# A new PE/DVE schedule for a fused linear-attention and softmax-attention kernel: exp pattern 2,2, background matmuls in pairs on a credit, a pool of free banks, and "warmer" matmuls

## Chip, cores, metric

One core of one Trainium2 chip. The metric is the device time of one execution in microseconds (us). The kernel before took 1404.0 us (median of 6 runs, 1399.91 to 1411.62).

Words used below: PE is the matmul engine, ACT the engine that does exp, DVE the vector engine, POOL the fourth engine. "Clock" is the granted TensorE clock as the profile gives it, as a share of full speed. In the traces of this case it is only ever 0.5 or 1.0, so a mean of 0.59 means 18% of the time at full clock. A "bank" is one of the eight buffers of 128 x 512 results that the matmuls write to; a "flow" is one sequence of background steps; a "unit" is the work of four heads on 512 queries; PV is the product of the exps with V; M0pad in the prediction is the tile of the bound for the exps, which enters the score matmul as its 17th row.

## The reference, cut to what matters

```python
# A: linear attention,  B: softmax attention; S=2048, D=512, H=32 heads of Dh=16 each
def _A_ref(x, wqkv, wo):
    q, k, v = ...                                   # x @ wqkv, by heads
    phi = lambda t: jnp.where(t > 0, t + 1, jnp.exp(t)) + 1e-6
    kv = einsum(phi(k), v); z = phi(k).sum over s
    return (phi(q) @ kv / (phi(q) @ z + 1e-6)) @ wo
def _B_ref(x, wqkv, wo):
    scores = einsum("bhqd,bhkd->bhqk", q, k) * Dh ** -0.5
    return (softmax(scores) @ v) @ wo
return concatenate([A, B], axis=-1)
```

B needs 32 x 2048 x 2048 exps, and the kernel has ACT do them. A and the projections are "background".

## The kernel before

The heads of B are handled in 8 groups of four. The scores are computed in tiles of 128 keys by 512 queries (2048 tiles). A score matmul contracts only 17 rows, so the four heads of a group sit in the four 32-row strips of the PE array, and their matmuls run at the same time. ACT takes the exp of 3 and of 2 score banks in turn. A PV group is four matmuls, each 32 columns of the array wide, also at the same time. The program decides once and for all in which order PE gets score, PV and background matmuls.

```python
NSC = 5                       # score banks
ACT_PATTERN = (3, 2)          # banks per exp
MISC_BANKS = tuple(range(NSC + 1, 8))     # two free banks for everything else
PE_BUDGET = 700.0; DVE_BUDGET = 1000.0
...
def make_S(n):                # one score tile: K=17 rows of strip j
    add("pe", mm(pf(b), KaT[32*j:32*j+17, gs, 128*kb:128*(kb+1)],
                 QaT[32*j:32*j+17, gs, 512*qb:512*(qb+1)], tp=(32*j, 0)), ...)
def make_PV(m):               # four matmuls, 32 columns each, into the accumulator bank
    ...
    if kb == NKB - 1:         # end of a unit (32 in all): evict, then the fp32 finish "fin"
        copy_task("dve", accs[:, u2, :], pf(ACC_BANK), ...)
        fin_flow[u] = start_flow(fin(g, qb, u), 0)
...
def prep(g):                  # background: K, Q, V of a later group, and a bound for the exps
    for t in range(4):
        yield (900.0, 650.0)                    # declared PE and DVE cost of the next step
        b = misc_bank()
        add("pe", _seq([mm(pf(b), wkp[:, gs, c, :], xTB[:, c, 512*t:512*(t+1)],
                        start=(c == 0), stop=(c == 3)) for c in range(4)]), ...)   # four in a row
    ...
    tt("pool", m0_f[...], prod[...], half_f[...], ALU.pow, ...)    # square root on POOL
...
def pump(scale):              # after each exp: let background flows go on
    pe_b = PE_BUDGET * scale; dve_b = DVE_BUDGET * scale
    fresh = True
    for f in list(flows):
        c = f["cost"]
        if (c[0] <= pe_b and c[1] <= dve_b) or fresh:   # the first step is always let through
            ...
            step_flow(f)
...
for i in range(NA):           # the main loop, one exp per turn
    add("act", exp of the next 3 or 2 banks)
    make_S(...)  ; make_PV(...) ; pump(ln / 3.0)
```

## Time and profile before

| | before |
|---|---|
| span of the profiled run | 1398.0 us |
| mean granted clock | 0.592 |
| PE / ACT / DVE / POOL busy | 79% / 71% / 20% / 15% |

First, lines of the profile page: the busy time and share of each engine; then the span in 40 slices, where a digit is tenths of busy time and PEclk is the clock in tenths; then the chain of work that ended last; then three groups of instructions (line, engine, operation, output<-inputs, shapes, count | busy us, mean ns of one | idle time before them and what ended it).

```profile
span 1398.0 us, 14809 instructions
PE 1109.4 (79%) x6520; PEld 362.2 (26%) x6520; DVE 280.7 (20%) x554; ACT 988.1 (71%) x875; POOL 212.3 (15%) x147
...
ACT  2265665675565667887688768887688768887885
...
PEclk8665555575565575555555565556555665555777
...
PE 46%; ACT 34%; POOL 10%; DVE 8%; issue 2%; ACTq 0%; POOLq 0%
...
L810 ACT ACTIVATE ring<-ps 128x1536 bf16<-128x1536 f32 (+1 forms) x819 | 959.8, 1250 | 275.9 <-PE ps L292 275.0
L292 PE MATMUL ps<-QaT,KaT 17*128 17x512 bf16 x2048 | 461.9, 561 | 166.1 <-ACT ring L810 165.9
...
L334 POOL TENSOR_TENSOR m_f<-prod,half_f 128x16 f32<-128x16 f32 x32 | 92.9, 2902 | 9.4 <-DVE prod L334 7.7
```

Neither ACT nor PE is full on average, and the clock is at half for most of the time. The average hides two stages. In a quiet stretch, without background, the timeline (start us, length us, engine, what; merged where contiguous) shows this:

```profile
739.17 5.57 ACT L810 ACTIVATE ring<-ps 128x1024 bf16<-128x1024 f32 x5
...
741.62 0.61 PE L292 MATMUL ps<-QaT,KaT 17*128 17x512 bf16 x3 [0.56 <-ACT ring L810]
...
742.16 0.62 PE L292 MATMUL ps<-ring,Va 128*32 128x512 bf16 x4
...
742.71 0.61 PE L292 MATMUL ps<-QaT,KaT 17*128 17x512 bf16 x2
...
743.88 0.61 PE L292 MATMUL ps<-QaT,KaT 17*128 17x512 bf16 x3 [0.56 <-ACT ring L810]
```

Here ACT runs without a gap, and PE, although at half clock, waits for it. Five tiles take 2.26 us (741.62 to 743.88). Count PE by the distance from start to start, since the ends overlap: a group of score matmuls holds PE for 0.54 us and a PV group for 0.55. With background it is PE that lacks time (PE alone, the clock rises within this stretch):

```profile
290.03 0.62 PE L292 MATMUL ps<-ring,Va 128*32 128x512 bf16 x4
290.58 1.89 PE L292 MATMUL ps<-xTB,wkp 128*128 128x512 bf16 x4
292.40 0.61 PE L292 MATMUL ps<-QaT,KaT 17*128 17x512 bf16 x3
292.94 0.62 PE L292 MATMUL ps<-ring,Va 128*32 128x512 bf16 x4
...
296.15 0.40 PE L292 MATMUL ps<-ring,Va 128*32 128x512 bf16 x4
296.48 1.04 PE L292 MATMUL ps<-xTB,wkp 128*128 128x512 bf16 x4
297.45 0.39 PE L292 MATMUL ps<-QaT,KaT 17*128 17x512 bf16 x2
297.77 1.21 PE L296 MATMUL ps<-ident_bf,arena 128*128 128x128 bf16 x16
```

At half clock four background matmuls hold PE for 1.82 us (290.58 to 292.40); at full clock 0.97 (296.48 to 297.45), PV 0.33 and scores 0.32. The clock is thus worth a factor of 1.7 to 1.9 on these three.

When does the clock rise? The Trainium skill ("TensorE: Matmul & The Clock Gate", Part 1, the HAM clock gate) says that PE's clock is halved by default and released after a busy window of 3413 ns, a window that runs freely. The clock records of this trace agree: only 0.5 and 1.0 occur, in multiples of 3413 ns. That part does not say what counts as busy. So I added up, for each such window of the trace, the columns that the matmuls streamed, weighted by the share of the array that they use (17 of 128 rows for a score matmul, 32 of 128 columns for a PV matmul, fp32 double), and divided by what full rate would have streamed. The weights and the threshold are a fit; the table has the windows of the loop, from the first score to the last PV:

| work of the window, share of full rate | windows (before) | of which the next window ran at full clock |
|---|---|---|
| under 0.34 | 299 | 0 |
| 0.34 to 0.36 | 19 | 0 |
| 0.36 to 0.38 | 12 | 8 |
| over 0.38 | 55 | 55 |

### The profile page before, as it was taken

Reading aid. Unit: us, or ns where it says so; the run is one execution under the profiler, and the core shown is the slowest. Engines: PE = TensorE matmul, PEld = TensorE weight load, DVE = VectorE, ACT = ScalarE, POOL = GpSimd, SP = SyncE. Lnnn points to the kernel's source line nnn. Section 1 sums busy time; section 2 is a strip of 40 time slices with the busy share of each in tenths; the row PEclk is TensorE's granted clock in tenths of the full one; section 3 lists DMA queues with packets and bytes.
Section 4 is the critical chain, followed back from the end, with each engine's and each line's share of the span. In section 5 each row is a group of like instructions: output and inputs, shape, how many; then the busy total and the mean of one; then the engine's idle time right before and its main releaser. Section 6 shows DMA issues by size and latency. Waiting matters only on the chain.

```text
span 1398.0 us, 14809 instructions
## 1 busy us (share of the span) xinstructions
PE 1109.4 (79%) x6520; PEld 362.2 (26%) x6520; DVE 280.7 (20%) x554; ACT 988.1 (71%) x875; POOL 212.3 (15%) x147
## 2 busy tenths in 40 slices
PE   5588787787888888778777877778777877778887
PEld 3223222233233233222312222222222232122222
DVE  6333222232244331002100110002100210000111
ACT  2265665675565667887688768887688768887885
POOL 4641111124100032001400050003200140000000
PEclk8665555575565575555555565556555665555777
DMA  7000000000000000000000000000000000000000
GB/s 241 1 1 0 1 0 0 0 1 0 0 14 17 24 8 1 0 0 0 1 1 0 1 1 0 0 1 1 0 1 0 1 1 0 0 0 8 16 16 23
DMA packets 11056, 13.53 MB, mean 10 GB/s; under 512 B 752, under 2 KB 9968, under 8 KB 10992
## 3 DMA queue, kind: packets, MB, share of 16 engines
q1 hardware_dynamic: 10992, 12.59, 2.6%
q8 instruction: 51, 0.84, 0.2%
q14 instruction: 13, 0.11, 0.0%
HBM read 8.39 MB, written 4.19 MB: 9 GB/s over the span
## 4 chain that ended last, share of the span: by engine, by line
PE 46%; ACT 34%; POOL 10%; DVE 8%; issue 2%; ACTq 0%; POOLq 0%
PE ps L292 42%; ACT ring L810 33%; POOL m_f L334 7%; PE ps L296 4%; DVE accs L302 2%; POOL qsq L334 1%; DVE tmpU L328 1%; POOL ksq L334 1%; ACT tmpE L343 1%; DVE o_tok L334 1%; DVE RlPad L302 1%; POOL M0pad L330 1%; DVE KaT L320 0%; DVE rden L340 0%; DVE rl_tok L340 0%
## 5 line engine op out<-in xcount | busy, mean ns | idle before, releaser
L810 ACT ACTIVATE ring<-ps 128x1536 bf16<-128x1536 f32 (+1 forms) x819 | 959.8, 1250 | 275.9 <-PE ps L292 275.0
L292 PE MATMUL ps<-QaT,KaT 17*128 17x512 bf16 x2048 | 461.9, 561 | 166.1 <-ACT ring L810 165.9
L292 PE MATMUL ps<-ring,Va 128*32 128x512 bf16 x2048 | 296.3, 570 | 1.0 <-ACT ring L810 1.0
L292 PEld LDWEIGHTS ps<-QaT,KaT 17*128 17x128 bf16 x2048 | 83.8, 98 | 497.8 <-ACT ring L810 434.8
L334 POOL TENSOR_TENSOR ksq<-KaT 128x1024 bf16<-128x1024 bf16 x16 | 30.2, 1892 | 625.6 <-DVE KaT L320 625.6
L302 DVE COPY accs<-ps 128x512 f32<-128x512 f32 x32 | 22.1, 691 | 489.2 <-PE ps L292 489.2
L292 PEld LDWEIGHTS ps<-ring,Va 128*32 128x32 bf16 x2048 | 56.1, 100 | 208.2 <-issue 206.2
L334 POOL TENSOR_TENSOR m_f<-prod,half_f 128x16 f32<-128x16 f32 x32 | 92.9, 2902 | 9.4 <-DVE prod L334 7.7
L292 PE MATMUL ps<-esel_f,accs 128*128 128x4 f32 x256 | 59.0, 354 | 26.2 <-DVE accs L302 26.2
L343 ACT ACTIVATE tmpE<-tmpU 128x512 f32<-128x512 f32 x32 | 20.1, 629 | 83.8 <-DVE tmpU L328 83.8
L292 PEld LDWEIGHTS ps<-esel_f,accs 128*128 128x128 f32 x256 | 56.2, 324 | 41.8 <-DVE accs L302 41.8
L292 PE MATMUL ps<-wA,arena 128*128 128x512 bf16 x128 | 55.3, 581 | 0.7 <-DVE kvacc L334 0.7
L292 PE MATMUL ps<-xTB,wqp 128*128 128x512 bf16 x128 | 45.5, 496 | 0.8 <-DVE o_tok L334 0.8
L292 PE MATMUL ps<-xTB,wkp 128*128 128x512 bf16 x128 | 45.1, 495 | 0.0
L296 PE MATMUL ps<-ident_bf,M0pad 128*128 128x128 bf16 x128 | 19.1, 304 | 30.8 <-POOL M0pad L330 30.8
L334 POOL TENSOR_TENSOR qsq<-QaT 128x1024 bf16<-128x1024 bf16 x16 | 30.2, 1892 | 70.7 <-DVE QaT L302 70.7
L296 PE MATMUL ps<-ident_f,RlPad 128*128 128x128 f32 x128 | 35.2, 430 | 5.9 <-DVE RlPad L302 5.9
L334 POOL TENSOR_TENSOR pk_n<-tmpW,tmpE 128x512 bf16<-128x512 f32 x16 | 20.2, 1262 | 128.4 <-ACT tmpE L343 128.3
L328 DVE TENSOR_SCALAR tmpU<-ps 128x512 f32<-128x512 f32 x32 | 22.1, 692 | 81.8 <-PE ps L292 81.8
L292 PE MATMUL ps<-wopad,arena 128*128 128x512 bf16 x128 | 37.4, 431 | 0.0
L334 POOL TENSOR_TENSOR pqT<-tmpW,tmpE 128x512 bf16<-128x512 f32 x16 | 20.2, 1263 | 86.8 <-ACT tmpE L343 80.4
L320 DVE TENSOR_SCALAR KaT<-ps,negc 128x512 bf16<-128x512 f32 x30 | 22.5, 751 | 46.2 <-PE ps L292 46.2
(102 smaller groups left out, 578.2 us busy)
## 6 DMA issues: line engine op xcount, KB each, us to landing
arena<-in_B_x_dram SPq DMA_DIRECT2D x4, 512.0 KB, 5.5
arena<-in_A_x_dram SPq DMA_DIRECT2D x4, 512.0 KB, 7.9
out_dram<-stA SPq DMA_DIRECT2D x16, 128.0 KB, 1.7
out_dram<-stB SPq DMA_DIRECT2D x16, 128.0 KB, 1.7
wB<-in_B_wqkv_dram SPq DMA_DIRECT2D x1, 1536.0 KB, 10.4
wA<-in_A_wqkv_dram SPq DMA_DIRECT2D x1, 1536.0 KB, 11.9
wopad<-in_B_wo_dram SPq DMA_DIRECT2D x4, 128.0 KB, 2.7
woA<-in_A_wo_dram SPq DMA_DIRECT2D x1, 512.0 KB, 3.6
```

Of the source, the lines that this page charges most:

```text
L292: return lambda e: e.matmul(o, l, r_, start=start, stop=stop, tile_position=tp, skip_group_check=sgc)
L296: return lambda e: e.transpose(o, i, ident)
L302: em = lambda e: e.tensor_copy(out=o, in_=i)
L320: em = lambda e: e.tensor_scalar(out=o, in0=i, scalar1=vec, scalar2=None, op0=ALU.add)
L328: em = lambda e: e.tensor_scalar(out=o, in0=i, scalar1=s1, scalar2=s2, op0=op0)
L330: em = lambda e: e.tensor_scalar(out=o, in0=i, scalar1=s1, scalar2=s2, op0=op0, op1=op1)
L334: return add(eng, lambda e: e.tensor_tensor(out=o, in0=i0, in1=i1, op=op), **kw)
L343: return add("act", lambda e: e.activation(out=o, in_=i, func=func), **kw)
L810: add("act", lambda e, b0=b0, ln=ln, rp=rp: e.activation(out=ring[:, 512 * rp:512 * (rp + ln)], in_=ps[:, 512 * b0:512 * (b0 + ln)], func= ...
```

## The change

The intent: at every exp, give PE exactly as much background as fits beside the exp, by a cost model that puts a 512-column matmul at 216 ns (the commonest distance between the starts of two such matmuls at full clock in the trace before); keep a third bank free; take the square root from POOL to DVE; and fill idle PE time with matmuls on zero weights ("warmers"), to keep its clock up. The core of the diff:

```diff
-NSC = 5
-ACT_PATTERN = (3, 2)
-RING = 10
+NSC = 4
+ACT_PATTERN = (2, 2)
+RING = 8
-PE_BUDGET = 700.0
-DVE_BUDGET = 1000.0
+T_EXP = {1: 490.0, 2: 916.5, 3: 1343.5, 4: 1770.0}
+T_MM = 216.0
+T_SLAT = 110.0
+PE_MARGIN = 100.0
+PE_MAX_BURST = 520.0
+PE_TARGET = 0.62
+DVE_SHARE = 0.9
...   # banks: try_bank / acquire / release instead of misc_bank, a flow waits until one is free
+        def pe_group(b, fs, r, per=2, cost=T_MM):     # a row of matmuls, cut into pairs
+            for k in range(0, len(fs), per):
+                if not first: yield (cost * len(ch), 0.0)
+                add("pe", _seq(ch), ...)
...   # prep: K, Q, V first, then the bound; the square root without POOL
-                tt("pool", m0_f[...], prod[...], half_f[...], ALU.pow, ...)
+            ts("dve", sq_y0[:].bitcast(I32), prod[:].bitcast(I32), 0.5, 532487669.0, ...)
+            recip(sq_r[:], sq_y0[:], ...)             # one Newton step
+            ...
...
+        def pump(pe_avail, dve_avail):
+            credit["pe"] = min(credit["pe"] + pe_avail, PE_MAX_BURST)
+            ...   # a step only goes if its cost is covered by the credit
+        def warmers(k):
+            if not acc_state["open"]: return
+            for _ in range(k):                        # adds zero to the open accumulator
+                add("pe", mm(pf(ACC_BANK), zeros_bf[:], xTB[:, 0, 0:512], start=False, stop=False,
+                             sgc=True), ...)
...
-            pump(ln / 3.0)
+            used = pump(t_per - main - PE_MARGIN, DVE_SHARE * t_per)
+            idle = PE_TARGET * t_per - main - used
+            if idle > 0.5 * T_MM:
+                warmers(int(idle / T_MM + 0.5))
```

Here `main` is 326 for a step with scores and 216 more with PV. A step without PV gets 490 of credit, one with PV 274, and the cap is 520. So one pair (432) goes per two steps, and a warmer comes only into a step with neither PV nor background.

## The prediction

> **What bounds the kernel now.** The span is 1398 us at a mean clock of 0.592 (list of cores). The page shows PE busy 79%, ACT 71%; the chain of waits is PE 46%, ACT 34%. The exp evictions cost 1461 ns (1536 columns) and 1038 ns (1024) and overlap by about 120 ns, so ACT alone would need some 926 us. In quiet groups (timeline, 741 to 755 us) ACT is at that floor, 2.26 us per five tiles, even at clock 0.50. The rest is bound by PE at half clock: a group of score matmuls holds PE for 0.54 us, a group of four PV matmuls 0.55, four 512-column background matmuls 1.82; at full clock they take 0.32, 0.33 and 0.97.
>
> **When the clock rises.** The Trainium skill ("TensorE: Matmul & The Clock Gate", the HAM clock gate) says that the clock is halved unless PE was busy in a free-running window of 3413 ns. The trace shows the same two states and window. Sorting the windows by matmul work (columns, weighted by the share of array cells used: a 17-row score matmul 0.13, a 32-column PV matmul 0.25) the next window ran at full clock where the work reached about 0.36 of full rate, and at half clock below, with few exceptions. Score and PV groups alone (about 0.2) never reach it.
>
> **What the change does.**
> - Pattern 3,2 becomes 2,2: 1024 score groups instead of 819. ACT floor 926 to 939 us (estimate). PE at half clock: 205 x 0.54 = 110 us more.
> - Background is cut into pairs, one pair per two steps, on credits that assume the full clock (216 ns). Two steps of score, pair, score, PV cost at half clock 0.54 + 0.96 + 0.54 + 0.55 = 2.6 us, against 1.83 us of exp; their work is 0.29 of full rate, below 0.36. The bursts that raised the clock before are gone, so I expect half clock nearly all through the loop.
> - Warmers: only steps with neither PV nor background get one, 128x512. That makes 0.25 to 0.29 of full rate: too little, while each costs 0.54 us of PE.
> - POOL's power function (32 x 2.9 us) leaves for small DVE operations; some 45 us of PE waits on M0pad go.
> - The fp32 finish (1.80 + 1.05 us of PE for each of 32 units) stays.
>
> **The sum** (estimate from these durations). PE at half clock in the loop: scores 551, PV 281, background and small matmuls about 370, fp32 92, warmers about 30: 1325 us. Waits on DVE, POOL and ACT fall from about 280 to about 130. Start and end 65. Full-clock stretches give back about 40. Total 1480 us. All of it is critical: PE becomes the bound even in quiet groups.
>
> **Predicted: 1480 us, 8 in 10 between 1330 and 1570. Faster by over 2%: 0.22; within 2%: 0.12; slower by over 2%: 0.66.**
>
> **Signs.** Right: mean clock 0.50 to 0.56; PE busy 85% or more and ACT about 65%, with ACT's idle time ended by PE score matmuls; about 2.6 us per two exps of 1024 columns in busy groups; ACT no longer saturated in late groups. Wrong: clock above 0.7, exps every 0.92 us over long stretches.
>
> **What would make it wrong.** If the monitor counts a warmer or a score group for more than I fitted, the clock stays up. Then PE needs only about 0.75 us per step, the loop becomes bound by ACT, and the time is 1080 to 1200 us.

## The result, and the profile after

The time is 1559.14 us (median of 8 runs, 1558.76 to 1560.88), against 1407.77 us before (16 runs of the same rounds). The ratio is 1.1077, with a 95% interval of 1.1052 to 1.1102. Ratios here are the mean time of one kernel's fast runs over that of the other's of the same rounds, so not quite the ratio of the medians.

The page after, the same lines as before:

```profile
span 1557.1 us, 15221 instructions
PE 1395.2 (90%) x6631; PEld 385.9 (25%) x6631; DVE 297.3 (19%) x598; ACT 1063.9 (68%) x1080; POOL 104.0 (7%) x79
...
ACT  2765656766567665667666676887788768887774
...
PEclk8555555555555555555555555555555555555556
...
PE 88%; DVE 8%; ACT 3%; issue 1%; POOL 0%; POOLq 0%
...
L880 ACT ACTIVATE ring<-ps 128x1024 bf16<-128x1024 f32 x1024 | 1036.0, 1022 | 343.5 <-PE ps L313 314.0
L313 PE MATMUL ps<-QaT,KaT 17*128 17x512 bf16 x2048 | 621.1, 603 | 74.4 <-ACT ring L880 74.3
...
L313 PE MATMUL ps<-xTB,zeros_bf 128*128 128x512 bf16 x111 | 67.4, 607 | 0.0
```

The clock is at half in every slice but the first and the last. The chain is 88% PE, where it had been shared between PE and ACT. The quiet stretch has changed sides:

```profile
1009.24 12.94 ACT L880 ACTIVATE ring<-ps 128x1024 bf16<-128x1024 f32 x12
...
1009.68 0.61 PE L313 MATMUL ps<-QaT,KaT 17*128 17x512 bf16 x2
...
1010.22 0.61 PE L313 MATMUL ps<-xTB,zeros_bf 128*128 128x512 bf16 x1
...
1010.76 0.61 PE L313 MATMUL ps<-QaT,KaT 17*128 17x512 bf16 x2
...
1011.30 0.62 PE L313 MATMUL ps<-ring,Va 128*32 128x512 bf16 x4
...
1011.85 0.61 PE L313 MATMUL ps<-QaT,KaT 17*128 17x512 bf16 x2
```

Score, warmer, score, PV: 2.17 us for four tiles (1009.68 to 1011.85), that is 0.54 us per tile, where it had been 2.26 us for five, 0.45 per tile. No wait is left on PE here, and ACT does one exp every 1.08 us (12 in 12.94 us), so ACT now waits for PE even without background. Two exps alone would take 1.83 us. With background, score, pair and score take the place of score, warmer and score:

```profile
305.89 0.61 PE L313 MATMUL ps<-QaT,KaT 17*128 17x512 bf16 x2
...
306.43 1.03 PE L313 MATMUL ps<-xTB,wqp 128*128 128x512 bf16 x2
...
307.39 0.61 PE L313 MATMUL ps<-QaT,KaT 17*128 17x512 bf16 x2
...
307.93 0.62 PE L313 MATMUL ps<-ring,Va 128*32 128x512 bf16 x4
```

I split PE's time in the loop, from the first score to the last PV, into slots and waits. A slot is the usual distance from the start of such a group to the start of the next; what a distance exceeds it by is a wait. The first and last column are computed so from the two traces (the split between slots and waits moves by some 10 us with the choice of the usual distance):

| us | before | predicted | after |
|---|---|---|---|
| scores (814, then 1023 groups) | 401 | 551 | 548 |
| PV | 261 | 281 | 281 |
| background and small matmuls | 270 | 370 | 368 |
| fp32 finish of the units | 89 | 92 | 95 |
| warmers | 0 | 30 | 60 |
| waits of PE | 297 | 130 | 145 |
| given back by full clock (already in the slots of the measured columns) | | -40 | none |
| start and end, outside the loop | 80 | 65 | 60 |
| total | 1398 | 1480 | 1557 |

In the loop before, 147 us of slots ran at full clock; after, none. Over the windows of the trace after, the work of a window (with the weights above) has a median of 0.26 and a maximum, outside start and end, of 0.344. None reaches 0.36.

### The profile page after: what moved, and what is told of

It is laid out like the page before. It is cut to its first block, busy times and chain, and to the rows that moved or that the text cites. A ratio compares the mean times of both kernels' runs of the same rounds, so it can differ in the third digit from the quotient of the medians.

```text
span 1557.1 us, 15221 instructions
## 1 busy us (share of the span) xinstructions
PE 1395.2 (90%) x6631; PEld 385.9 (25%) x6631; DVE 297.3 (19%) x598; ACT 1063.9 (68%) x1080; POOL 104.0 (7%) x79
## 4 chain that ended last, share of the span: by engine, by line
PE 88%; DVE 8%; ACT 3%; issue 1%; POOL 0%; POOLq 0%
PE ps L313 83%; PE ps L317 5%; ACT ring L880 2%; DVE accs L323 1%; DVE tmpU L349 1%; ACT tmpE L364 1%; DVE RlPad L323 1%; DVE o_tok L355 1%; DVE rl_tok L361 1%; DVE xTB L333 0%; DVE iota_t L349 0%; DVE sq_r L361 0%; DVE sq_t L355 0%; DVE mask_f L349 0%; DVE M0pad L351 0%
## 5 line engine op out<-in xcount | busy, mean ns | idle before, releaser
L880 ACT ACTIVATE ring<-ps 128x1024 bf16<-128x1024 f32 x1024 | 1036.0, 1022 | 343.5 <-PE ps L313 314.0
L313 PE MATMUL ps<-QaT,KaT 17*128 17x512 bf16 x2048 | 621.1, 603 | 74.4 <-ACT ring L880 74.3
L313 PE MATMUL ps<-ring,Va 128*32 128x512 bf16 x2048 | 315.7, 608 | 0.0
L313 PEld LDWEIGHTS ps<-QaT,KaT 17*128 17x128 bf16 x2048 | 105.5, 99 | 546.6 <-issue 292.1
L313 PE MATMUL ps<-xTB,zeros_bf 128*128 128x512 bf16 x111 | 67.4, 607 | 0.0
L313 PE MATMUL ps<-xTB,wkp 128*128 128x512 bf16 x128 | 63.6, 610 | 0.0
L313 PE MATMUL ps<-xTB,wqp 128*128 128x512 bf16 x128 | 61.5, 590 | 0.0
L313 PE MATMUL ps<-wopad,arena 128*128 128x512 bf16 x128 | 56.4, 562 | 0.0
L323 DVE CAST QaT<-ps 128x512 bf16<-128x512 f32 x30 | 20.8, 692 | 111.9 <-PE ps L313 111.9
L313 PE MATMUL ps<-wB,xTB 128*128 128x64 bf16 x512 | 36.1, 235 | 0.0
```

The source lines that it names most:

```text
L313: return lambda e: e.matmul(o, l, r_, start=start, stop=stop, tile_position=tp, skip_group_check=sgc)
L323: em = lambda e: e.tensor_copy(out=o, in_=i)
L880: add("act", lambda e, b0=b0, ln=ln, rp=rp: e.activation(out=ring[:, 512 * rp:512 * (rp + ln)], in_=ps[:, 512 * b0:512 * (b0 + ln)], func= ...
```

## The experiments

Theory A: PE at half clock is the bound after the change; the stream is too thin to raise the clock, and the 2,2 pattern and the warmers add slots at that clock. The rivals are named with each run. All runs were correct. All times are medians unless it is said otherwise; the kernel before, run beside them, took 1403.55 to 1404.05 us.

**1. No warmers** (`e1_nowarmers`).

```diff
-            if idle > 0.5 * T_MM:
+            if False:
                 warmers(int(idle / T_MM + 0.5))
```

> The changed kernel without its 111 warmer matmuls. Theory A (PE at half clock is the bound; the warmers are too thin to raise the clock): clock stays at 0.51, and the time falls a little, because a quiet cycle of two exps drops from 2.17 us (four PE slots of 0.54) to the 1.83 us of the exps: 111 x 0.34 = 38 us, so about 1520 us. Rival B (the warmers' own PE slots are the main loss): the time falls by well over 60 us. Rival C (the warmers help): the clock falls further or the time rises.

Measured: 1526.2 us (1525.65 to 1526.69), ratio 1.0894, clock 0.511. The warmers cost 33 us and didn't hold up the clock at all. Rivals B and C fall.

**2. The kernel before with 32-row scores** (`e2_before_rows32`). The added rows of K and Q are zeros; the matmul streams the same 512 columns.

```diff
-            add("pe", mm(pf(b), KaT[32 * j:32 * j + 17, gs, 128 * kb:128 * (kb + 1)],
-                         QaT[32 * j:32 * j + 17, gs, 512 * qb:512 * (qb + 1)], tp=(32 * j, 0)),
+            add("pe", mm(pf(b), KaT[32 * j:32 * j + 32, gs, 128 * kb:128 * (kb + 1)],
+                         QaT[32 * j:32 * j + 32, gs, 512 * qb:512 * (qb + 1)], tp=(32 * j, 0)),
```

> The kernel before, with the score matmuls fed 32 rows instead of 17 (the 15 extra rows of K and Q are zeros, so the result is the same and each matmul has the same 512 columns). If the clock monitor counts active rows, score work counts 0.25 instead of 0.13 of full rate, some 0.04 to 0.1 more per window, windows that missed the threshold now pass it, and the clock rises from 0.59 to about 0.64 to 0.70, with 1320 to 1370 us. Rival: if it counts only time or whole 32-row tiles, clock 0.59 and 1404 us unchanged.

Measured: 1363.84 us (1362.27 to 1367.39), ratio 0.9739 [0.969, 0.9787]; clock 0.628 in the profiled run. The clock rose, by a little less than expected, and the time fell by 40 us, on nothing but rows of zeros. So active rows count for the clock. Taking the windows of both kernels together, one threshold (0.365) puts 17 of 760 windows on the wrong side if the scores are weighted 17/128 and 32/128, and over 30 if both get the same weight of 0.13, 0.19 or 0.25. A recount gives over 30 as well if a PV matmul gets half or double its weight, each with its best threshold. The weights and the threshold as they stand put 79 of the 5588 loop windows of all fourteen traces on the wrong side.

**3. The changed kernel with the old 3,2 pattern** (`e3_pattern32`).

```diff
-NSC = 4
-ACT_PATTERN = (2, 2)
-RING = 8
+NSC = 5
+ACT_PATTERN = (3, 2)
+RING = 10
```

> The changed kernel with the old pattern: exps of 3 and 2 banks, 5 score banks, 2 free banks, ring of 10. Theory A: 205 score groups of 0.54 us go, 110 us of PE at half clock, so about 1450 us at clock 0.50 to 0.53. Rival D (the new bank pool is what matters, two free banks choke it): no gain or a loss, with PE waiting for DVE. Rival E (the pattern is the whole loss): 1405 us or less.

Measured: 1471.96 us (1470.26 to 1472.01), ratio 1.0504, clock 0.511. The score slots fell by 108 us (548 to 440), as expected. Some 20 us of it came back as warmers: 148 instead of 111, since the longer exp leaves more room by the cost model. The waits stayed (about 149 us, working with the full count of matmuls, since this trace lacks 1.6% of their records). So two free banks did not choke it (rival D), and the pattern is a large loss, but not the whole (rival E).

**4. More warmers** (`e5_hot`).

```diff
-PE_TARGET = 0.62
+PE_TARGET = 0.90
...
                 warmers(int(idle / T_MM + 0.5))
+            if done % 64 == 8:
+                warmers(12)
```

> The changed kernel with several hundred more warmers: target 0.90 instead of 0.62, and 12 in a row at the start of each of the 32 units. Theory A: the row of 12 lifts the work of a window over the threshold, the denser stream then holds it, clock 0.8 or more, PE slots fall from 0.54 to 0.33 us, and though PE has more work the time falls to 1130 to 1280 us. Rival F (work on zero weights doesn't count for the clock, or the clock is not the bound): clock about 0.5 and every warmer costs 0.43 to 0.54 us, so 1850 us or more.

Measured: 1555.01 us (1554.73 to 1556.64), clock 0.731. Time and clock missed both expectations. The clock did rise, so work on zero weights counts. PE did 954 warmers more (1065 against 111 weight loads of zeros) and was no slower in sum. The timeline shows what full clock is worth; the row of 12 starts at half clock and ends at full:

```profile
714.32 4.17 PE L313 MATMUL ps<-xTB,zeros_bf 128*128 128x512 bf16 x12 [0.24 <-issue]
...
718.42 0.39 PE L313 MATMUL ps<-QaT,KaT 17*128 17x512 bf16 x2
...
718.74 0.60 PE L313 MATMUL ps<-xTB,wkp 128*128 128x512 bf16 x2
...
718.85 16.61 ACT L880 ACTIVATE ring<-ps 128x1024 bf16<-128x1024 f32 x18 [4.45 <-PE ps L313]
```

After it ACT did 18 exps in 16.61 us without a gap, 0.92 us each, with the background of a preparation beside them. But ACT had waited 4.45 us for that row, and in a later window with little matmul work (here a unit's finish, before 747.9 us) the clock fell again, as it did 31 times in the loop; at half clock the warmers cost 0.43 to 0.54 us each. A little under half of the PE slots ran at full clock. What that won (score and PV slots fell from 829 to about 626 us, background too), the warmers lost: they held PE for about 330 us instead of 60, half of it at half clock. The dose by itself thus bought nothing.

**5. Background in rows of four again** (`e4_bursts`), and **the same without warmers** (`e9_bursts_nowarmers`).

```diff
-        def pe_group(b, fs, r, per=2, cost=T_MM):
+        def pe_group(b, fs, r, per=4, cost=T_MM):     # a first row of four is charged as two
-PE_MAX_BURST = 520.0
+PE_MAX_BURST = 1000.0
```

> The changed kernel with its background matmuls again in rows of four, charged as two, and a credit limit of 1000 instead of 520, so that rows can follow each other in successive steps. Theory A (the bursts were what raised the clock before): a stretch of score, row of four, score, PV, row of four does about 0.38 of full rate even at half clock, over the 0.36 of the fit, so the clock rises again, to 0.55 to 0.65 in the mean, and the time falls by 40 to 120 us from 1557. Rival: clock 0.51, and only the 16 us of saved weight loads.

Measured: 1595.95 us (1590.46 to 1600.49), clock 0.553. The clock rose as expected, and the time rose too: a miss. Background was done sooner, so more steps were quiet and got a warmer: 305 instead of 111, at half clock. To test that:

> The burst variant (1596 us, clock 0.55) without warmers. It had 302 warmers instead of 111, since background finished earlier and quiet steps get warmers. Theory A: each of the 190 extra ones lengthened a quiet pair of exps from 1.83 to 2.17 us, which hid what the risen clock gave; without any, 302 x 0.34 = 100 us less, 1490 us, at clock 0.54 to 0.57, that is 20 to 60 us under the changed kernel without warmers (1526). Rival: bursts in themselves cost time, then it stays over 1526 us.

Measured: 1510.52 us (1509.87 to 1514.93), ratio 1.0784, clock 0.554. The warmers had cost 85 us, so they were what made the burst variant slower. Against no warmers without bursts (1526) 16 us are left, less than expected: PE's slots fell by some 95 us (1292 to 1197), but its waits rose by some 80 (171 to 252). By the list of waits, half of the rise is PE waiting for ACT's exps (85.6 to 127.6 us); why, was not separated.

**6. 32-row scores in the changed kernel** (`e6_after_rows32`), the edit of experiment 2.

> The changed kernel with 32-row score matmuls. The fit says that the stream at half clock then does 0.30 (quiet) to 0.33 (busy) of full rate, best windows about 0.36: at the threshold, mostly under it. Clock 0.51 to 0.57, time within 4% below 1557 us. If it rises over 0.65, the fit of the threshold is off.

Measured: 1559.71 us (1559.13 to 1559.88), clock 0.512. There is no effect at all, as the fit says for a stream that stays at or below the threshold (best loop window 0.373, none followed by full clock). What gave 40 us before the change gives nothing after it.

**7. Dependent steps held back** (`e8_holds`). A step may name a number of schedule steps for which it is not to be emitted; nothing else is edited (125 warmers came out of it instead of 111).

```diff
+                f["hold"] = pumps[0] + (f["cost"][2] if len(f["cost"]) > 2 else 0)
...
-                    if f not in flows:
+                    if f not in flows or f["hold"] > pumps[0]:
                         continue
...
-            yield (4 * 80.0, 450.0)          # unit's finish, waits for DVE's copy
+            yield (4 * 80.0, 450.0, 3)
-            yield (4 * 80.0, 0.0)            # needs the squares from POOL
+            yield (4 * 80.0, 0.0, 6)
...   # and eleven more places of this kind
```

> The changed kernel where steps that depend on a DVE, POOL or ACT result are held back by 2 to 6 schedule steps, so that the in-order PE and ACT don't wait for them. Nothing else. The 145 us of PE waits in the loop fall to 40 to 80 us; PE slots stay; clock stays 0.51; so 1460 to 1500 us. Rival G (waits are the main loss and also what keeps the clock down): clock above 0.6 and time under 1400 us.

Measured: 1427.04 us (1425.98 to 1427.4), ratio 1.0188, clock 0.514. The waits fell from 145 to 12 us, further than expected, so the time is below the expected range; the slots stayed (1352 and 1355 us). It is still some 1.9% over the kernel before. Rival G falls. The page of this run is the plainest picture of theory A: a PE that never waits, at half clock.

```profile
span 1425.5 us, 15237 instructions
PE 1395.0 (98%) x6645; PEld 389.0 (27%) x6645; DVE 295.3 (21%) x598; ACT 1064.3 (75%) x1080; POOL 103.7 (7%) x79
...
PEclk8555555555555555555555555555555555555556
...
PE 97%; DVE 2%; ACT 0%; issue 0%; POOL 0%; POOLq 0%
```

It also settles an obvious rival to the fit, that the time PE is busy sets the clock: in 390 of the 399 loop windows of this trace PE was busy for over 95% of the window, and none was followed by full clock.

**8. All together, warmers dosed by the threshold** (`e7_warm`): the edits of experiments 6 and 7, and

```diff
-            idle = PE_TARGET * t_per - main - used
-            if idle > 0.5 * T_MM:
-                warmers(int(idle / T_MM + 0.5))
+            if done % 4 == 0:                      # every second step
+                warmers(max(0, int((WORK - used_prev - used) / T_MM + 0.5)))    # WORK = 430
+            if done % 64 == KICK_AT:
+                warmers(KICK)                      # 6 in a row, once per unit
+            used_prev = used
...   # warmers go to a free bank while the accumulator is closed
```

> All together: 32-row scores, steps held back, warmers so dosed that every two steps hold two full matmuls' worth beside scores and PV (0.46 of full rate), also while the accumulator is closed, and a row of six once per unit. Theory A: the clock rises at the start and nothing drops it: 0.9 or more; exps then follow each other every 0.92 us, 939 us for the loop plus about 20 us of phi exps, 60 us of start and end and up to 100 us of rests: 1060 to 1180 us. If the clock still drops at each unit, 1250 to 1400 us.

Measured: 1189.84 us (1184.43 to 1198.13), ratio 0.8501 [0.8454, 0.8547], clock 0.86 in the profiled run. It is just above the expected range; the clock still dropped 20 times in the loop.

**9. The dose mended** (`e10_warm2`), **with 17 rows** (`e11_warm2_rows17`), **and without any warmer** (`e12_nofill`). The first counts the real matmul work of a step instead of its charge, and holds back the first matmul of a preparation. The second is the same with 17 rows, the third the same without warmers and rows of six.

```diff
                         if f["pri"] > 0:
-                            used += c[0]
+                            used += WORK_OF.get(c[0], 0.0)   # 426, 427 or 213; small and fp32 steps 0
-            yield (200.0, 100.0)
+            yield (200.0, 100.0, 3)
```

> The warm variant (1190 us, clock 0.86) with the dose mended: the matmul work of a step is counted as it is, not by its credit, since the 22 drops of the clock fell on stretches where steps of little work (four columns wide) had been charged 320; and the first matmul of a preparation is held until its weights are copied. Theory A: few drops are left, clock 0.93 or more, 1090 to 1140 us.

> The same with 17-row scores, that is with 0.055 less of full rate per window (0.41 instead of 0.46 in a quiet pair, threshold 0.36), and only 0.29 while cold, so that the row of six has to lift more. Theory A: more drops, clock 0.70 to 0.90, 1130 to 1280 us. If the rows didn't matter, the same time as with 32.

> The same with 32 rows, without any warmer: only the held-back steps are left against the changed kernel. Theory A: the clock stays down, 0.51 to 0.56, PE at half clock is the bound, 1350 to 1420 us; the distance to the version with warmers, 250 us or more, is what the clock is worth. Rival: warmers only fill, the time is within 5% of the version with them.

| run | median of all runs, us | fast runs, us | their clock | expected us |
|---|---|---|---|---|
| e10_warm2 | 1183.12 | 1155.47, 1168.69 | 0.88 to 0.90 | 1090 to 1140 |
| e11_warm2_rows17 | 1306.3 | 1296.77 to 1313.42 (all four) | 0.72 to 0.74 | 1130 to 1280 |
| e12_nofill | 1382.27 | 1360.04, 1380.01 | 0.52 to 0.54 | 1350 to 1420 |

The other runs of the first and the last are marked slow, being over 1.5% above the fastest of their kernel; their clock goes with their time (0.86 and 0.51). I take it that where the free-running window falls decides it, but no run shows that. The ratios to before, by the fast runs, are 0.8291, 0.9316 and 0.9775 (the last unclear at 2%). The profiled run of e10 is one of the slow ones (1182.56 us, clock 0.865).

The order of the three is as theory A has it: with the same attention work, the fast runs have means of 1370, 1306 and 1162 us from the lowest clock to the highest. Only the one without warmers is inside its expected range; the other two were too hopeful. The rows matter now (144 us), where they did nothing in experiment 6. The clock is worth about 208 us here, less than the 250 expected. The mending brought some 28 us against experiment 8. The clock still dropped 17 times in the loop of the profiled run, each time but two after a window of under 0.36. The timeline shows two kinds of such windows. First, around a drop at 634.4 us:

```profile
632.25 0.65 ACT L367 ACTIVATE tmpE<-tmpU 128x512 f32<-128x512 f32 x1
632.44 0.39 PE L316 MATMUL ps<-QaT,KaT 32*128 32x512 bf16 x2 [0.53 <-ACT ring L895]
```

ACT does an exp of A's phi between two score exps, and PE waits. Ten of the 17 drops followed a window with such an exp and a PE wait of about 0.53 us or more. Second, PE around a drop at 1003.1 us:

```profile
1002.15 0.40 PE L316 MATMUL ps<-ring,Va 128*32 128x512 bf16 x4
1002.48 1.35 PE L316 MATMUL ps<-esel_f,accs 128*128 128x4 f32 x8
1003.69 0.59 PE L316 MATMUL ps<-xTB,zeros_bf 128*128 128x512 bf16 x1
```

The fp32 finish of a unit holds PE for over 1 us (1002.48 to 1003.69) with matmuls of four columns, which by the fit count for nearly nothing. Six of the 17 drops followed a window with part of a finish. Warmers laid around both, or a finish without fp32, would be the next step; it was not tried.

## Why the prediction was wrong

The direction and the mechanism held. Predicted were half clock nearly all through the loop (0.50 to 0.56; measured 0.512), PE busy 85% or more (90%), ACT about 65% (68%), 2.6 us per two exps in busy stretches (305.89 to 307.93 is score, pair, score in 2.04, and a PV slot of 0.55 makes 2.6), and late groups no longer bound by ACT (2.17 us per four tiles). The alternative, 1080 to 1200 us if the clock stayed up, did not come from the change. It came nearly true when the dose was set by the threshold and 32-row scores and held-back steps were added (1190 us in experiment 8, 1162 in the fast runs of experiment 9); more warmers alone did not bring it (experiment 4). So it was the dose and the waits around it that failed, and not the idea.

The size was wrong: 1480 us, and 1557 in the trace. The step that failed is "The sum", in these terms:

- "Full-clock stretches give back about 40": none did. No slot of the loop ran at full clock. I had supposed that the clock would be up at the start of the loop and in the flush, and didn't check this against the threshold: with 0.29 for the busy stream of pairs, it never gets up at all. 40 us.
- "warmers about 30": 60 us, 111 of them. I had guessed how many quiet steps would be left. 30 us.
- "Waits on DVE, POOL and ACT fall from about 280 to about 130": 145 us. 15 us.
- Scores, PV, background and fp32 were 1294 us in the sum and 1292 in the trace; start and end 60 instead of 65.

These make up the 77 us between 1480 and 1557. A further fault lies in what I made of a wait: I had noted that PE became the bound everywhere, and yet left the waits at a round 130 us, though on a PE that is the bound each of them adds to the time. Experiment 7 took 133 us of them away and the time fell by 132 us.

What the change as a whole did, by the parts shown: the 2,2 pattern cost about 87 us (experiment 3) and the warmers 33 (experiment 1); all full clock of the loop was lost, and restoring the rows of four brings back part of it (0.554 against 0.592 before, experiment 5); and the change won part of the time back, since PE, having become the bound, waits for ACT less (waits 297 to 145 us), and the start is 20 us shorter. That the shorter start comes from the square root on DVE was not tested alone.

## What to carry to other kernels

Before costing a schedule, find out at which PE clock it will run: add up the matmul work of each clock window, weighted by the rows and columns of the array in use, and compare it with the threshold of that trace. A schedule that spreads background thinly may lose the clock that bursts had raised, and a filler matmul is either dosed past the threshold, held there through every wait, or it is a plain cost. When one in-order engine becomes the bound, every place where it waits for another engine is on the critical path, and holding dependent work back by a few steps can be worth as much as removing work (here 132 us for 133 us of waits).

## What the Trainium skill lacked or had wrong

- "TensorE: Matmul & The Clock Gate", Part 1: it does not say what counts as activity. Columns count here, by the fit weighted by active rows and columns of the array: in the trace before 0 of 318 loop windows under 0.36 of full rate raised the clock or kept it up, 63 of 67 over it did, and in experiment 7 a PE busy for 98% of the span had a mean clock of 0.514; 15 more rows of zeros per score matmul raised the mean clock from 0.59 to 0.63 and cut 40 us (experiment 2). Part 4 of the page says that transposes don't count in the same way; here leaving the bf16 transposes out of the sum puts 29 instead of 17 windows of experiment 2's two traces on the wrong side.
- The same page and part: its table of states gives an idle window as what throttles again; its passage on PSUM-queue cycling has short idles between matmuls do it too, without a figure. Here a window at a third of full rate was enough. In `e10_warm2` the window of 3413 ns from 999.7 us, in which the lines shown above begin, did 0.35 of full rate with no PE wait over 0.26 us, and the next window ran at half clock; so did those after the windows from 713.0 and 777.8 us, at 0.34 of full rate and with no PE wait at all.
- The same page: it does not say whether matmuls on zero weights count for this clock. They do: 954 more of them took the mean clock from 0.51 to 0.73 (experiment 4).
- "ScalarE: Activation LUTs", section "What ACT_TABLE_LOAD costs": 186 ns + 0.833 ns per column, for an instruction with immediate scale and bias, gives 1039 ns for 1024 columns; the trace before has 1038. It says that back-to-back instructions overlap by about 93 ns; here 18 exps of 1024 columns in 16.61 us follow each other every 0.92 us, an overlap of about 0.12 us.
